# Two decode layers on one core: the order of the loads at the change of layers, and w4's last pieces

## The chip, the cores and the metric

One core of a Trainium2 chip. The metric is the device time of one execution in microseconds; below it also appears as the span, from the first to the last instruction in the trace.

## What is computed

One token passes through four steps: attention A, mixer B, A again, B again, with the same weights and the same K and V caches both times. So there are two layers of A and B, and everything is read from memory twice.

```python
# A: x (1,1,640); 32 heads of 192; the last W = 4096 of 32768 cached positions
q = (x @ wq).reshape(B, Sq, Hq, Dh) ...
k = k_cache[:, :, Sk - W:, :];  v = v_cache[:, :, Sk - W:, :]
p = softmax(einsum("bhqd,bhkd->bhqk", q, k) * Dh ** -0.5)
return einsum("bhqk,bhkd->bhqd", p, v) ... @ wo        # wo (6144, 640)
# B: with one position the four shifted parts are all zero, so hs = 0 and x1 = x
h2 = gelu(layernorm(x1) @ w3) @ w4                     # w3 (640, 1536), w4 (1536, 640)
return x1 + h2
# all: x = x + A(layernorm(x)); x = x + B(layernorm(x)); and both once more
```

## The kernel before

**Storage.** SBUF holds twelve cells of 1536 KB (128 partitions x 6144 bf16). A cell takes K or V of one head, or w3, w4 or a piece of wo. `take` (L147) gives the cell that has been free longest, `give` (L152) puts one back. Both run while the program is written, so the cell that a load gets is fixed, and so is the last reader of that cell's tenant before it, for which the load waits. Eight transposed K (heads 0 to 7) stay in their cells from layer 0 to layer 1, so layer 1 starts with work that needs no load. V of head 3 (`VC`) stays too. V of head 2 (`VP`) stays elsewhere, one part in PSUM: in layer 1 it has no load at all, but it needs a cell into which VectorE turns it back (`v_words`, L591, the transposes at L599). V of head 4 (`VX`) stays in part, so that layer 1 loads 864 KB of it. Most of w3 and w4 lies in a cell, the rest in a fixed tile `wx_sb` (one k-block of w3, three blocks of w4), which is loaded only in layer 0.

**Order of the loads.** All loads are issued by SyncE (SP), one after another, in the order of a written list, `layer_stream` (L246). `need` (L290) walks that list as far as the load asked for. An issue that waits holds up all behind it. Each transfer counts on one of eight counters in turn, so it also waits until the eighth transfer before it has landed.

**Change of layers.** Layer 0 ends with w3 and w4 in the mixer (`load_w3`, `load_w4`, `mixer`), then layer 1 begins. Its first takers of cells, in the order of the list, are v0 and v1 (V of heads 0 and 1), which get the cells of w3 and w4; then v2, then k8, v4 and k9. The scores of heads 0 to 3 (L494, called through `S`, L701) free one cell of a kept K each, in that order. In the kernel before, v2 gets head 0's cell, k8 head 1's, v4 head 2's; head 3's becomes a work area, and k9 gets head 4's.

**Computation.** TensorE makes the scores (L494), V's product (L610) and the projections; VectorE transposes K (L418) and the products (L617); ScalarE makes the exponentials. In the mixer, L942 multiplies by w3, L954 to L975 form the gelu, and L989 multiplies by w4: twelve blocks of five matmuls each. In layer 0 the order of the blocks is: eight in the cell, three in `wx_sb`, and last the ninth in the cell, a block of 160 KB that is loaded by itself (L238). L996 then makes x of the next layer. In layer 1 it is: the three in `wx_sb`, the eight in the cell, and the ninth; L994 makes the result, L1010 and L1012 turn it, and SP writes it (L1013).

Of the kernel before, what the change touches and what calls it, by code (L numbers as in the profile page):

```python
# [59 lines left out]
def kernel(  # L60
# [14 lines left out]
    nc = tc.nc  # L75
    shrink_ring(nc)
    _, _, D = A_x.shape
# [10 lines left out]
    QH = 4  # L88
# [17 lines left out]
    VC, VP, VX, VW, VN = 3, 2, 4, 20 * Dh // 2, (NKL + NKX) * Dh  # L106
    assert NA * D + FREE - 2 * VW <= FREE

    W3C, W4C = FREE // F, FREE // D
# [37 lines left out]
    def take(key):  # L147
        i = free.popleft()
        cell_of[key] = i
        return (low if i == NCELL - 1 else cells).tile([P, FREE], BF16, tag=f"cell{i}", name=f"cell{i}")  # L150
# [73 lines left out]
    def load_w4(layer):  # L224

        t = take(("w4", layer))
        nx, x0 = NF - W4C, (ND - W3C) * F
        pairs = B_w4.rearrange("(k p two) n -> p k (two n)", p=P, two=2)
        ones_ = B_w4.rearrange("(k p two) n -> p k two n", p=P, two=2)
        h = W4C // 2  # L230
        n = h if layer == 0 else h // 2
        for k in range(0, h, n):
            nc.sync.dma_start(t[:, 2 * k * D:2 * (k + n) * D].rearrange("p (k n) -> p k n", k=n),
                              pairs[:, 2 + k:2 + k + n, :])
        if layer == 0:
            nc.sync.dma_start(wx_sb[:, x0:x0 + 2 * D], pairs[:, 0, :])
            nc.sync.dma_start(wx_sb[:, x0 + 2 * D:x0 + 3 * D], ones_[:, 1, 0, :])
        nc.sync.dma_start(t[:, 2 * h * D:W4C * D], ones_[:, 1, 1, :])  # L238
        blocks = [wx_sb[:, x0 + k * D:x0 + (k + 1) * D] for k in range(nx)]
        blocks.append(t[:, 2 * h * D:W4C * D])  # L240
        blocks += [t[:, k * D:(k + 1) * D] for k in range(2 * h)]
        return blocks
# [3 lines left out]
    def layer_stream(layer):  # L246
        groups = GROUPS[layer]
        seq, later = [], []

        def k_item(hh):  # L250
            if layer == 0 or hh >= NKEEP:
                seq.append(("k", layer, hh))

        def v_item(hh):
            if (layer, hh) == (1, VC):
                return
            if (layer, hh) == (1, VP):
                later.append(("v", layer, hh))
                return
            seq.append(("v", layer, hh))  # L260

        if layer == 0:
            for hh in groups[0]:
                k_item(hh)
        for gi, cur in enumerate(groups):
            nxt = list(groups[gi + 1]) if gi + 1 < len(groups) else []
            late = gi + 2 >= len(groups)
            for i, hh in enumerate(cur):
                if nxt:
                    k_item(nxt.pop(0))  # L270
                if nxt and late and i == 2:
                    k_item(nxt.pop(0))
                v_item(hh)
                if later and i == QH - 1:
                    seq.append(later.pop())
                if layer == 0 and gi + 1 == len(groups) and i < 2:
                    seq.append(("wo", layer, groups[gi + i - 1][0] // QH))
            if gi + 2 < len(groups) and gi >= layer:
                seq.append(("wo", layer, cur[0] // QH))
        if layer == 1:  # L280
            for g in groups[-2:]:
                seq.append(("wo", layer, g[0] // QH))
        seq.append(("w3", layer))
        seq.append(("w4", layer))
        return seq

    stream = [("wq", 0, 0), ("x",)] + [("wq", 0, kc) for kc in range(1, ND)] + layer_stream(0) + layer_stream(1)
    pos = [0]

# [611 lines left out]
    def mixer(layer, x_cur, z, rs_cur, ss_cur, x_new, rs_new):  # L901
# [81 lines left out]
        y2_ps = psm.tile([P, ND], F32, tag="psm")  # L983
        n = NF - W4C
        fcs = list(range(n)), list(range(n + 1, NF))
        fcs = (fcs[1] + fcs[0] if layer == 0 else fcs[0] + fcs[1]) + [n]
        order = [(n, fc) for fc in fcs for n in range(ND)]
        for i, (n, fc) in enumerate(order):
            nc.tensor.matmul(  # L989
# [13 lines left out]
    zs = [const.tile([P, 1], F32, name=f"zs{i}") for i in range(4)]  # L1003
    attention(0, xT, rs0, x1, z[0], zs[0], zs[1])
    mixer(0, x1, z[0], zs[0], zs[1], x2, rs2)
    attention(1, x2, rs2, x3, z[1], zs[2], zs[3])
    mixer(1, x3, z[1], zs[2], zs[3], x4, None)

    row_ps = psm.tile([ND, P], out.dtype, tag="psm")
# [34 lines left out]
```

## Time and profile before

| what | value |
|---|---|
| median of three runs | 514.91 us (514.85 to 515.27) |
| the profiled execution | 513.87 us, span 512.1 us |
| TensorE busy | 326.1 us, 64% of the span; mean granted clock 0.682 |
| VectorE busy | 290.9 us, 57% |
| ScalarE busy | 48.8 us, 10% |
| DMA | 215.11 MB, mean 420 GB/s over the span |
| chain that ended last | wo 3.8% of the span, w4 2.0%, then L989, L994, L1010, L1012 |

How it is read: the page cuts the span into 40 slices of 12.8 us and gives for each the busy share of every engine in tenths, the clock that was granted to TensorE, the share of the 16 DMA engines and what they moved. Behind it stand questions to the trace: rows in order of time (start, duration, engine, line, operation, out<-in, number, and in brackets the idle time ahead of it with what ended it); the waits in total (engine, line, what was waited for: us in total, times, longest); and busy times by stretches. SPq is SP's DMA queue; the time of a transfer is given from issue to landing, and a transfer has landed when the last of the DMA engines has finished its part.

### The profile page before, as it was taken

The page shows a single profiled execution, that of the slowest core. Times are in us where ns is not written, and L with a number is a line of the kernel's source. Part 1 is how long each engine was busy: PE and PEld are TensorE (multiplying, and loading weights), DVE is VectorE, ACT ScalarE, POOL GpSimd, SP SyncE. Part 2 cuts the span into 40 slices and gives each one's busy share as a digit, 9 for nine tenths or more (in the row PEclk, how much of TensorE's full clock was granted, in tenths as well). Part 3 has the DMA queues.
Part 4 walks back from the last instruction along what each step waited for, and adds up shares of the span by engine and source line. Part 5 has one row for each costly group of instructions (what it writes and reads, how often), then busy time and mean ns, then how long its engine had stood idle before and what let it go on. Part 6 is the DMA issues. An engine that isn't in the chain of part 4 may idle for free. (4 is left out here: it accounts for less than half of the span.)

```text
span 512.1 us, 9455 instructions
## 1 busy us (share of the span) xinstructions
PE 326.1 (64%) x4084; PEld 191.4 (37%) x4084; DVE 290.9 (57%) x587; ACT 48.8 (10%) x173; POOL 4.0 (1%) x16
## 2 busy tenths in 40 slices
PE   1057657666566645857655767667676766767765
PEld 0023334333333323534333544434343443434435
DVE  2067667676565755467623245666576566756622
ACT  1000101010010100101011111001010100100011
POOL 2000000000000000000000000000000000000000
PEclk9999878567665776576675585675565577656765
DMA  8999999999999999999999999999999999999996
GB/s 369 430 430 427 432 439 430 439 427 415 454 433 427 434 408 425 430 416 451 428 403 417 351 444 427 424 436 420 434 427 420 430 439 427 424 439 430 419 407 240
DMA packets 11997, 215.11 MB, mean 420 GB/s; under 512 B 2548, under 2 KB 3060, under 8 KB 7412
## 3 DMA queue, kind: packets, MB, share of 16 engines
q1 hardware_dynamic: 11956, 214.51, 98.4%
q8 instruction: 32, 0.52, 0.4%
q14 instruction: 9, 0.07, 0.0%
HBM read 214.50 MB, written 0.00 MB: 419 GB/s over the span
## 5 line engine op out<-in xcount | busy, mean ns | idle before, releaser
L494 PE MATMUL ST_ps<-cell,Qblk 128*16 128x256 bf16 x1536 | 161.3, 378 | 102.7 <-DVE cell L418 67.9
L418 DVE STREAM_TRANSPOSE cell<-cell 128x768 uint32<-128x768 uint32 x224 | 200.4, 944 | 11.7 <-DMA cell<-in_A_k_cache_dram 11.5
L494 PEld LDWEIGHTS <-Qblk 128*16 128x16 bf16 x1536 | 84.7, 111 | 171.6 <-issue 145.8
L610 PE MATMUL O_ps<-cell,PT 128*2 128x384 bf16 x1010 | 101.5, 473 | 7.2 <-DMA cell<-in_A_v_cache_dram 5.2
L617 DVE STREAM_TRANSPOSE o_sb<-O_ps 128x384 f32<-128x384 f32 x64 | 37.2, 581 | 112.5 <-PE O_ps L610 112.3
L610 PEld LDWEIGHTS <-PT 128*2 128x2 bf16 x1024 | 46.5, 102 | 22.5 <-issue 13.6
L553 DVE STREAM_TRANSPOSE o_sb<-o_sb 128x256 bf16<-128x256 bf16 x16 | 7.1, 445 | 33.9 <-ACT o_sb L548 24.7
L625 ACT ACTIVATE oT<-oT_ps,rl 32x6 bf16<-32x6 f32 x40 | 10.3, 257 | 158.7 <-PE oT_ps L624 150.4
L624 PE MATMUL oT_ps<-o_sb,Lq 128*32 128x6 f32 x160 | 14.0, 196 | 11.2 <-DVE o_sb L617 10.6
L624 PEld LDWEIGHTS oT_ps<-o_sb,Lq 128*32 128x32 f32 x160 | 12.9, 145 | 21.7 <-issue 16.1
L630 ACT ACTIVATE oT<-oT_ps,rl 32x6 bf16<-32x6 f32 x24 | 6.2, 257 | 110.3 <-PE ST_ps L494 95.1
L448 PE MATMUL qT_ps<-xc,wq_sb 128*128 128x1 bf16 x210 | 7.2, 165 | 12.9 <-DMA wq_sb<-in_A_wq_dram 12.1
L437 PE MATMUL qr_ps<-wq_sb,xc 128*1 128x384 bf16 x90 | 13.5, 452 | 0.0
L564 PE MATMUL PT_ps<-o_sb,Eq 128*32 128x32 bf16 x256 | 7.2, 237 | 9.2 <-DVE o_sb L553 4.0
L462 DVE TENSOR_TENSOR Xq<-qT_ps,maskq 128x24 bf16<-128x24 f32 (+1 forms) x18 | 2.9, 159 | 17.9 <-PE qT_ps L448 17.5
L448 PEld LDWEIGHTS <-wq_sb 128*128 128x128 bf16 x210 | 6.8, 104 | 14.1 <-DMA wq_sb<-in_A_wq_dram 13.1
L569 PE MATMUL l_ps<-lh,ones 128*128 128x4 f32 x32 | 8.5, 336 | 4.9 <-ACT PT L567 4.9
L564 PEld LDWEIGHTS <-Eq 128*32 128x32 bf16 x256 | 5.4, 109 | 16.5 <-issue 16.4
L545 ACT COPY nb_sb<-nb_ps 128x1 f32<-128x1 f32 x16 | 2.5, 159 | 93.8 <-PE nb_ps L542 93.8
L656 PE MATMUL yr_ps<-cell,oT 128*1 128x320 bf16 x108 | 11.4, 357 | 0.0
L542 PEld LDWEIGHTS nb_ps<-ones,o_sb 1*128 1x128 f32 x32 | 7.3, 283 | 7.4 <-issue 5.5
L629 PE MATMUL oT_ps<-o,Lq 128*32 128x6 f32 x48 | 6.2, 201 | 6.0 <-DVE o L628 6.0
(146 smaller groups left out, 196.7 us busy)
## 6 DMA issues: line engine op xcount, KB each, us to landing
cell<-in_A_k_cache_dram SPq DMA_DIRECT2D x56, 1536.0 KB, 26.4
cell<-in_A_v_cache_dram SPq DMA_DIRECT2D x56, 1536.0 KB, 26.4
cell<-in_A_wo_dram SPq DMA_DIRECT2D x13, 960.0 KB, 24.5
wq_sb<-in_A_wq_dram SPq DMA_DIRECT2D x5, 1536.0 KB, 12.1
cell<-in_A_v_cache_dram SPq DMA_DIRECT2D x6, 768.0 KB, 23.1
cell<-in_A_v_cache_dram SPq DMA_DIRECT2D x2, 864.0 KB, 9.0
cell<-in_B_w_dram SPq DMA_DIRECT2D x1, 1536.0 KB, 11.8
cell<-in_B_w_dram SPq DMA_DIRECT2D x2, 768.0 KB, 10.2
```

Source lines behind the costliest of these rows:

```text
L418: nc.vector.transpose(Tu, Ku[:, :, q * NY:(q + 1) * NY])
L437: nc.tensor.matmul(qr_ps[32 * i:32 * i + 1, :], lhsT=xc[:, kc:kc + 1], rhs=wq_sb[:, kc, t0 * P + i * N:t0 * P + (i + 1) * N], start=(kc == ...
L448: nc.tensor.matmul(qT_ps[:, tl:tl + 1], lhsT=wq_sb[:, kc, t * P:(t + 1) * P], rhs=xc[:, kc:kc + 1], start=(kc == 0), stop=(kc == ND - 1))
L494: nc.tensor.matmul(ST_ps[r:r + QW, :].rearrange("p (g i) -> p g i", g=ng), lhsT=Q[:, n, :], rhs=T4[:, :, f, :, t], start=(hq == 0 and n == ...
L542: nc.tensor.matmul(nb_ps[:], lhsT=held["w"], rhs=ones[0:1, 0:1], start=True, stop=True)
L564: nc.tensor.matmul(PT_ps[32 * m:32 * (m + 1), :, :, ng * q:ng * (q + 1)], lhsT=Eq[:, q, :], rhs=src[:, m:QW:NM], start=True, stop=True)
L569: nc.tensor.matmul(l_ps[:], lhsT=ones[:], rhs=held["lh"][:], start=True, stop=True)
L610: nc.tensor.matmul(O_ps[r:r + 2, :], lhsT=PT[:, hq, 2 * i:2 * i + 2], rhs=v_pair(V, h, 2 * i * Dh, 2 * Dh), start=(i < 4), stop=(i >= NB - 4))
L617: nc.vector.transpose(o_sb[:], O_ps.rearrange("p (e a c) -> p e c a", e=2, c=NA))
L624: nc.tensor.matmul(oT_ps[r, :], lhsT=Lq[:], rhs=o_sb[:, e, :, e], start=(e == 0), stop=(e == 1))
L625: nc.scalar.activation(oT[r, :], oT_ps[r, :], ACTF.Copy, scale=rl[r, 0:1])
L656: nc.tensor.matmul(yr_ps[32 * i:32 * i + 1, :], lhsT=oT[:, k:k + 1], rhs=wo_t[:, k * D + i * N:k * D + (i + 1) * N], start=(k == 0), stop= ...
```

## The change

Three edits:

- In `layer_stream` the place of v2 in layer 1 moves: it was put behind the last head of the first group (heads 0 to 3), so ahead of k8, and now follows V of head 4. So k8 takes head 0's cell, v4 head 1's and v2 head 2's. As v2 has no load, the order of the issues stays; what changes is which cell each waits for.
- In layer 0 the load of w4's ninth block goes ahead of the two loads into `wx_sb`, and the matmuls follow: eight blocks in the cell, the ninth, then the three in `wx_sb`.
- In layer 1 w4's eight blocks come in three loads (640, 320 and 320 KB) where they came in two of 640 KB; the ninth block follows as before. The order of its matmuls is the same.

On TensorE the same 60 matmuls of the mixer stand in another order in layer 0; nothing else moves on TensorE, VectorE, ScalarE or GpSimd. SP has one issue more, in the last mixer.

```diff
@@ load_w4
         h = W4C // 2
-        n = h if layer == 0 else h // 2
-        for k in range(0, h, n):
+        k = 0
+        for n in (h,) if layer == 0 else (h - 2, 1, 1):
             nc.sync.dma_start(t[:, 2 * k * D:2 * (k + n) * D].rearrange("p (k n) -> p k n", k=n),
                               pairs[:, 2 + k:2 + k + n, :])
+            k += n
+        nc.sync.dma_start(t[:, 2 * h * D:W4C * D], ones_[:, 1, 1, :])
         if layer == 0:
             nc.sync.dma_start(wx_sb[:, x0:x0 + 2 * D], pairs[:, 0, :])
             nc.sync.dma_start(wx_sb[:, x0 + 2 * D:x0 + 3 * D], ones_[:, 1, 0, :])
-        nc.sync.dma_start(t[:, 2 * h * D:W4C * D], ones_[:, 1, 1, :])
@@ layer_stream
                 v_item(hh)
-                if later and i == QH - 1:
+                if later and seq[-1] == ("v", layer, VX):
                     seq.append(later.pop())
@@ mixer
         fcs = list(range(n)), list(range(n + 1, NF))
-        fcs = (fcs[1] + fcs[0] if layer == 0 else fcs[0] + fcs[1]) + [n]
+        fcs = fcs[1] + [n] + fcs[0] if layer == 0 else fcs[0] + fcs[1] + [n]
```

## The prediction

> **What bounds the kernel now.** I read the page's slices first, then the waits of the two computing engines by stretch, then the issues of SP's DMA queue, then the end. All times are of the profiled execution.
>
> ```profile
> DMA  8999999999999999999999999999999999999996
> GB/s 369 430 430 427 432 439 430 439 427 415 454 433 427 434 408 425 430 416 451 428 403 417 351 444 427 424 436 420 434 427 420 430 439 427 424 439 430 419 407 240
> ```
>
> The DMA engines are busy from end to end and mostly move 420 to 440 GB/s. The change takes away no byte, so it can only win where the stream falters: slice 22 (351 GB/s, 282 to 294 us) is the change of layers, the last slice is the end. Is the computation a second bound? This is every wait of TensorE and VectorE for a DMA between 286 us and the end:
>
> ```profile
> PEld L942 <- DMA cell<-in_B_w_dram: 0.9, 1, 0.9
> PE V_ps L942 <- DMA cell<-in_B_w_dram: 0.8, 1, 0.8
> PEld L989 <- DMA cell<-in_B_w_dram: 0.2, 1, 0.2
> PE y_ps L989 <- DMA cell<-in_B_w_dram: 0.2, 1, 0.2
> ```
>
> So in layer 1 the computation never waits for data until w3's second half. Two chains run side by side, **the transfers** and **the computation**; they meet at L942, where the transfers are 0.83 us late. This caps the case: whatever the seam gives to the transfers, the end moves by 0.83 us there and no further, because then the computation is the bound.
>
> The seam, by stretches (the last three columns are granted clock, DMA share, GB/s):
>
> ```profile
> 282.00:287.00 5.00, 2.70 (x71) 2.43 (x69) 2.08 (x16) 1.16 (x5) 0.00 (x0) 0.50 0.97 374
> 287.00:298.00 11.00, 9.75 (x239) 7.01 (x242) 3.57 (x12) 0.76 (x4) 0.00 (x0) 0.76 0.93 349
> 298.00:304.00 6.00, 3.87 (x86) 2.72 (x84) 2.21 (x10) 1.08 (x4) 0.00 (x0) 0.88 1.12 466
> 304.00:312.00 8.00, 5.76 (x72) 2.58 (x64) 1.78 (x4) 0.77 (x3) 0.00 (x0) 0.50 0.99 426
> ```
>
> Against the 426 GB/s that follow, 287 to 298 lost 11 x (1 - 349/426) = 2.0 us and 298 to 304 gave back 6 x (466/426 - 1) = 0.6: **1.4 us** net, as a mean over the engines.
>
> **What the change moves at the seam.** These are head 0's scores, the issues of v1, k8 and v4 (V and K of layer 1, by head), and head 1's and 2's scores:
>
> ```profile
> 285.93 0.33 SPq L156 DMA_DIRECT2D cell<-in_A_v_cache_dram  x1
> ...
> 288.28 1.46 PE L494 MATMUL ST_ps<-cell,Qblk 128*16 128x256 bf16 x24 [0.30 <-DVE Qblk L477]
> ...
> 289.80 1.46 PE L494 MATMUL ST_ps<-cell,Qblk 128*16 128x256 bf16 x24
> ...
> 291.30 0.33 SPq L156 DMA_DIRECT2D cell<-in_A_k_cache_dram  x1
> ...
> 291.70 1.15 PE L494 MATMUL ST_ps<-cell,Qblk 128*16 128x256 bf16 x24
> ...
> 292.90 0.33 SPq L181 DMA_DIRECT2D cell<-in_A_v_cache_dram  x1
> ```
>
> Each issue stands 0.04 to 0.05 us behind the end of the scores that free its cell: k8 behind head 1's (289.80 + 1.46 = 291.26), v4 behind head 2's (291.70 + 1.15 = 292.85). Head 0's cell goes to v2, which has no load: it is filled from PSUM by L599. After the change the three cells go to k8, v4, v2 in turn.
>
> 1. **k8** is issued behind head 0's scores: 288.28 + 1.46 + 0.04 = 289.78, or 1.52 us earlier. **v4** is issued behind head 1's, 291.30, or 1.60 earlier. Nothing is added to SP; k9 keeps its cell and its issue at 295.88, and so do all behind it.
> 2. **v2's** cell comes free at 292.85 and not at 289.74. L599 writes it at 294.82, behind the instruction before it on VectorE (L477, 294.64), so 1.97 us cover it; with the cover gone the softmax's first maximum (L519, 298.79) would be late behind it on VectorE after another 1.6 us.
> 3. **w4 of layer 0.** v1 waits for w4's cell: its waits are 1.6 us for w4's last block and then 0.3 for L989. The block that lands last there (160 KB, issued 275.44) now goes ahead of the 320 and 160 KB that are bound for another tile, and its five matmuls go ahead of those 15. The cell's last matmul ends 15 matmuls sooner (285.10 to 285.61: 0.51 us), so v1 is issued at about 285.4. The 60 matmuls stay 60; the 320 KB block lands behind 160 KB more, at about 284.75 + 0.4 = 285.15, and TensorE reaches it at 285.10 + 5 x 0.034 = 285.27. I cost this at nothing; with the cover of 0.12 gone x2, and so the computation, would be some 0.1 us late.
>
> How much do the transfers gain? By issue plus time to landing, k8 lands at 299.6 (291.30 + 8.3), v4 at 301.9, k9 at 305.6, v5 at 309.2: a full load takes 3.6 us in a full queue, v4's 864 KB 2.0. The trace has no k8 issued into this queue earlier, so I bound it. Upper end: v0, issued into a nearly empty queue, took 7.3 us; k9 by that row lands at 295.88 + 7.3 = 303.2 at the soonest, 2.4 us sooner. Lower end: only v1's shift counts, 0.5. A loss below nothing I exclude, since no load is issued later than before. I take **1.5 us**, the shift of k8 that v4 and k9 follow and near the 1.4 of the bytes. Does it last to the end? From 304.80 on loads land 15 us and more behind their issue (26.4 in the median), so the queue stays filled and a lead is kept. What arrives at the end is then 1.5 us, of which **0.83 us** count.
>
> **The end.** w4 of layer 1 came as 640, 640 and 160 KB and now comes as 640, 320, 320 and 160.
>
> ```profile
> 505.25 0.48 PE L942 MATMUL V_ps<-xc,cell 128*128 128x1 bf16 x12 [0.83 <-DMA cell<-in_B_w_dram]
> ...
> 507.63 0.67 PE L989 MATMUL y_ps<-hT,cell 128*128 128x1 bf16 x20
> ...
> 508.46 0.82 PE L989 MATMUL y_ps<-hT,cell 128*128 128x1 bf16 x25 [0.16 <-DMA cell<-in_B_w_dram]
> 509.32 0.16 DVE L994 TENSOR_TENSOR x<-base,y_ps 128x5 bf16<-128x5 f32 x1 [1.32 <-PE y_ps L989]
> ```
>
> Twenty-five matmuls stand behind the second 640 KB, which lands at 497.97 + 10.4 = 508.4. With it in halves, the first lands about 0.75 us sooner (half the 1.5 us between 506.9 and 508.4, the landings of the two 640 KB pieces), and ten matmuls x 0.033 fill the wait and run past 508.4. But TensorE is busy on both sides of the wait, so the gain is the wait alone, **0.16 us**, not the 0.33 of ten matmuls. The added issue costs SP 0.34 us beside the 9.8 us that it then waits for the result. A transfer is not issued before the eighth ahead of it has landed, so one more also pushes the last block one place on: it waits for the landing that SP's last instruction now waits 0.8 us for, and goes out at about 500.3 instead of 499.12. The rate holds until 504 us, so some 3.5 us cover it; uncovered it would cost 1.2.
>
> The 640 KB pieces land 1.5 us apart and the 160 KB block 0.4 behind the last (508.8), each at about 420 GB/s. So I see no price per transfer in a filled queue. The Trainium skill speaks against the change here: "DMA: Bandwidth & Descriptors", section "Anatomy of one DMA", puts about 2.0 us fixed on each transfer (for transfers issued from GpSimd), and its "Bandwidth" section asks for 1 MiB or more. By it the sum would be 1 us slower; the rows just given disagree with it.
>
> **Sum**: -0.83 - 0.16 = **-1.0 us** against the profiled 513.87 (span 512.1 and 1.8 around it). The median of the runs shown, 514.91, stands 1.0 above that execution; I take the same difference from it: **513.9**. A measurement of this kernel can tell about 0.2%, 1.03 us, from no change, so the forecast stands just at that line.
>
> **Rivals.**
> - *The seam gives little.* For it: the DMA share over 287 to 298 is 0.93, only 0.8 us idle, and v1's shift alone is 0.5. Then 0.3 to 0.6 us come through and 0.16 at the end: 514.2 to 514.5. Chance 0.20.
> - *The computation is already the bound in the runs that are timed*, which are 1.0 us longer than the profiled one. Then the seam is hidden and only the end is left: 514.75. Chance 0.12.
> - *The computation gets shorter*, because the clock's steps fall better on it. The granted clock in 286 to 296 is a mean of 0.68, in 296 to 303 it is 0.97; 24 score matmuls take 1.46 us in the slow part and 0.87 in the fast one (293.62). One step of some 3.4 us more at full clock is worth up to 1.4. With the transfers' 1.5 that ends near 513.2. Chance 0.10.
> - *Slower: the same clock falls worse.* The place is TensorE between 292 and 303 us, now at a mean clock of 0.97 and busy for 8.1 of the 11 us; 8.1 x (1.46/0.87 - 1) = 5.5 us are at stake. The computation has 0.83 us of slack, so slower begins where more than that plus 0.16 is lost, and by over 0.2% from 2.0 us on. Half of it lost gives 2.7 - 0.83 - 0.16 = +1.7: 516.6. Against it: the change moves no matmul there by more than 0.1 us. Chance 0.05. "TensorE: Matmul & The Clock Gate" in the Trainium skill, section "Part 1", says that the clock follows activity in free-running windows of 3.4 us; by that a step can fall otherwise in any execution, changed or not.
> - *Slower: each transfer has a fixed price at the end.* The nearest row is the result's write into an empty queue, 510.09 to 512.1: +2.0 - 1.0, 515.9. Chance 0.03; the landings 0.4 us apart speak against it. This is where the DMA page's rule would lead.
>
> **Chances and range.** Forecast 0.50, rivals 0.50 as given. Of the forecast about half (0.24) passes 1.03 us, which with the shorter computation makes faster 0.34; same is 0.26 + 0.20 + 0.12 = 0.58; slower 0.08. The range, 513.1 to 514.9, takes in all but the slower cases and the far part of the shorter computation.
>
> **What would show it.** k8's issue near 289.8, v4's near 291.3, v1's near 285.4, k9's unchanged near 295.9; over 350 GB/s between 287 and 298; k9 landed before 305; L942 with no wait for w3 or a short one; no wait inside the last 45 matmuls of L989. Wrong would be: issues moved but landings not (the loss isn't in the queue), or L942 still waiting 0.8 us (the lead was given back on the way).

## The result, and the profile after

The kernel after takes **512.81 us** (median of five runs, 512.72 to 514.16); before took 515.27 beside it (514.85 to 515.39). The ratio is **0.9967 with a 95% interval of 0.9952 to 0.9982**, so it is faster by 0.33%. The forecast was 513.9, in a range from 513.1 to 514.9: the median lies 0.3 us below the range; from the 514.91 that the forecast started from, this ratio leads to 513.2, inside it. Two more comparisons of the same kernel gave 0.9977 (0.9964 to 0.9990) and 0.9986 (0.9967 to 1.0004), with medians of 513.17 and 513.56. A ratio is not quite the quotient of the two medians beside it; where the two differ, the ratio is used. Weighted by their intervals the three ratios make 0.9976 (0.9967 to 0.9984), or 1.2 us.

The profiled execution of after is the 512.81 one, with a span of 511.0 us. Behind L236 its line numbers are one higher: L942 is now L943, L989 is L990, L638 is L639, L494 is L495. The slices of the page, for after:

```profile
DMA  8999999999999999999999999999999999999996
GB/s 369 431 431 428 433 440 431 440 428 415 444 433 401 435 428 441 431 407 457 429 391 417 380 438 432 421 428 441 432 425 431 432 424 431 428 426 435 424 403 246
```

The slice of the change of layers, which had 351 GB/s, now has 380; the others scatter, by up to 26 GB/s down and 21 up. The stretches of the seam (clock, DMA share, GB/s last) and SP's issues (start, duration; the first row holds v0 and v1, then k8, v4 and k9):

```profile
282.00:287.00 5.00, 2.65 (x71) 2.46 (x70) 2.10 (x16) 1.27 (x7) 0.00 (x0) 0.50 0.98 381
287.00:298.00 11.00, 9.24 (x246) 6.47 (x247) 3.54 (x11) 0.63 (x4) 0.00 (x0) 0.81 1.01 385
298.00:304.00 6.00, 3.87 (x86) 2.75 (x78) 2.21 (x10) 1.08 (x4) 0.00 (x0) 0.78 1.11 466
```

```profile
281.75 3.84 SPq L156 DMA_DIRECT2D cell<-in_A_v_cache_dram  x2
289.60 0.33 SPq L156 DMA_DIRECT2D cell<-in_A_k_cache_dram  x1
291.11 0.33 SPq L181 DMA_DIRECT2D cell<-in_A_v_cache_dram  x1
295.22 0.48 SPq L55 DMA_DIRECT2D cell<-in_A_k_cache_dram  x1
```

The issues stand where the prediction put them: k8 at 289.60 (289.78 foreseen), v4 at 291.11 (291.30), v1 at 285.27 by its own row (285.4). Only k9, foreseen unchanged at 295.88, went 0.66 us earlier, because the clock's step came earlier and the scores ahead of it were shorter (head 2's took 0.86 us for 1.15). In another profiled execution of after it went at 295.86. The stream between 287 and 298 us no longer falters: its share is 1.01 after 0.93.

Now the waits of TensorE and VectorE for a DMA from 286 us on, all of them, and the end of the kernel:

```profile
PEld L943 <- DMA cell<-in_B_w_dram: 1.2, 2, 1.0
PE V_ps L943 <- DMA cell<-in_B_w_dram: 0.9, 1, 0.9
PEld L639 <- DMA cell<-in_A_wo_dram: 0.4, 1, 0.4
PE y_ps L639 <- DMA cell<-in_A_wo_dram: 0.3, 1, 0.3
```

```profile
498.28 1.53 PE L639 MATMUL y_ps<-oT,cell 128*128 128x1 bf16 x45
500.08 0.70 PE L639 MATMUL y_ps<-oT,cell 128*128 128x1 bf16 x15 [0.28 <-DMA cell<-in_A_wo_dram]
...
504.24 0.48 PE L943 MATMUL V_ps<-xc,cell 128*128 128x1 bf16 x12 [0.92 <-DMA cell<-in_B_w_dram]
...
506.63 1.50 PE L990 MATMUL y_ps<-hT,cell 128*128 128x1 bf16 x45
```

The wait inside w4's last 45 matmuls is gone. But L943 still waits 0.92 us for w3's second half, although the transfers came 1 us sooner. So the computation came sooner as well: L639, the last output projection, begins at 498.28 and not at 500.43, and now waits for wo itself. The prediction had read the computation as a second bound that would stop the gain at 0.83 us. That is what the experiments had to settle. One more row belongs to the end, the write of the result, before and after:

```profile
510.09 0.30 SPq L1013 DMA_DIRECT2D out_dram<-Lb  x1
```

```profile
508.93 0.30 SPq L1014 DMA_DIRECT2D out_dram<-Lb  x1
```

From its issue to the end of the span it is 2.01 us before and 2.11 after.

### The profile page after: what moved, and what is told of

It is laid out like the page before. It is cut to its first block, busy times and chain, and to the rows that moved or that the text cites. A ratio compares the mean times of both kernels' runs of the same rounds, so it can differ in the third digit from the quotient of the medians.

```text
span 511.0 us, 9455 instructions
## 1 busy us (share of the span) xinstructions
PE 324.9 (64%) x4084; PEld 191.4 (37%) x4084; DVE 291.3 (57%) x587; ACT 48.9 (10%) x173; POOL 4.0 (1%) x16
## 4 chain that ended last, share of the span: by engine, by line
DMA 58%; PE 20%; DVE 17%; issue 2%; ACT 1%; SPq 1%; DVEq 0%; ACTq 0%
DMA cell<-in_A_k_cache_dram 34%; DMA cell<-in_A_v_cache_dram 20%; DVE cell L419 12%; PE ST_ps L495 9%; PE O_ps L611 6%; DMA cell<-in_B_w_dram 4%; DVE o_sb L618 2%; PE qT_ps L449 1%; PE y_ps L990 1%; DVE pm L520 1%; PE nb_ps L543 1%; DVE o_sb L554 1%; PE l_ps L570 1%; PE pmT_ps L525 1%; DVE V_ps L600 1%
## 5 line engine op out<-in xcount | busy, mean ns | idle before, releaser
L495 PE MATMUL ST_ps<-cell,Qblk 128*16 128x256 bf16 x1536 | 161.8, 379 | 101.8 <-DVE cell L419 66.7
L495 PEld LDWEIGHTS <-Qblk 128*16 128x16 bf16 x1536 | 85.0, 111 | 171.4 <-issue 145.0
```

Of the source, the lines that this page charges most:

```text
L495: nc.tensor.matmul(ST_ps[r:r + QW, :].rearrange("p (g i) -> p g i", g=ng), lhsT=Q[:, n, :], rhs=T4[:, :, f, :, t], start=(hq == 0 and n == ...
```

## The experiments

**Theory A**: the transfers set the end, and the gain is the lead that they take at the change of layers. **Theory B**: the computation sets the end in the runs that are timed, and after is faster because TensorE's clock falls better on it.

The table puts the profiled executions beside each other. The first two columns of numbers are the stream's rate and TensorE's granted clock between 287 and 298 us. "k10" is the mean landing, over the 16 DMA engines, of K of head 10, the second K load behind k8; "mean" and "last" are the landings of w3's second half over the 16 engines (a transfer has landed with the last); the start is that of the matmuls that wait for it, at L942 in before; the last column is the span less that start.

| profiled execution | GB/s | clock | k10 | mean | last | start (wait) | span | span less start |
|---|---|---|---|---|---|---|---|---|
| before | 349 | 0.76 | 311.0 | 503.4 | 505.2 | 505.25 (0.83) | 512.1 | 6.8 |
| before, again | 337 | 0.78 | 311.6 | 503.8 | 506.8 | 506.85 (0.93) | 513.7 | 6.9 |
| cells only | 366 | 0.79 | 310.4 | 502.8 | 504.1 | 504.17 (0.56) | 511.1 | 6.9 |
| w4 of layer 0 only | 365 | 0.78 | 310.8 | 503.3 | 505.2 | 505.26 (1.21) | 512.0 | 6.7 |
| cells and w4 of layer 0 | 374 | 0.82 | 310.2 | 502.7 | 504.1 | 504.17 (0.92) | 511.0 | 6.9 |
| last pieces only | 325 | 0.70 | 311.8 | 504.2 | 507.0 | 507.09 (0.92) | 513.9 | 6.8 |
| cells later | 308 | 0.50 | 312.0 | 504.5 | 506.2 | 506.20 (0.88) | 513.1 | 6.9 |
| after | 385 | 0.81 | 310.2 | 502.7 | 504.2 | 504.24 (0.92) | 511.0 | 6.8 |
| after, again | 374 | 0.53 | 310.9 | 503.4 | 505.8 | 505.85 (0.93) | 512.7 | 6.8 |
| after, third | 428 | 0.78 | 310.1 | 502.5 | 505.4 | 505.47 (0.93) | 512.3 | 6.8 |
| after, less load | 381 | 0.75 | 310.0 | 500.6 | 502.4 | 504.45 (none) | 511.1 | 6.6 |
| after, less computation | 377 | 0.51 | 311.8 | 504.2 | 505.7 | 505.74 (0.92) | 512.5 | 6.8 |
| after, both less | 367 | 0.53 | 311.3 | 501.9 | 504.1 | 504.13 (0.92) | 510.9 | 6.8 |

In all rows but one, w3's second half starts at most 0.1 us behind its landing, and the kernel ends 6.7 to 6.9 us later. One landing sets the end; the exception is the run with fewer bytes.

The table also shows that a lead from the seam arrives whole. From k10's mean landing to w3's the stream takes 192.3 to 192.5 us in all eleven rows with all bytes, whatever the kernel and the clock, and 190.6 us in the two with 768 KB less. What is gained or lost up to k10 is still there 192 us later.

### The cells alone

```diff
-                if later and i == QH - 1:
+                if later and seq[-1] == ("v", layer, VX):
```

> Only the twelfth cell changes hands. Theory A (the lead of the transfers at the change of layers does it): k8 issued near 289.8 and v4 near 291.3 with v1 still near 285.9; the stream over 287 to 298 us rises from 349 towards 375 GB/s; w3's second half lands 0.6 to 0.9 us sooner and the time falls by most of what the whole change gave, 1.2 to 1.8 us. Theory B (the computation of layer 1 bounds the timed runs and the change only happened to meet better clock steps): issues move as said, but the time stays within 0.5 us of before.

Measured: 514.38 us against 515.06 before, ratio 0.9991 (0.9972 to 1.0010): no difference that can be told, and less than the 1.2 to 1.8 us that theory A had led to expect; this timing alone fits theory B as well. In the trace k8 went at 289.92, v4 at 291.43 and v1 at about 286.07, so the rewired cells do what the diff says. By the means over the engines, k9 landed at 303.06 after 303.66 and 304.08 in the two profiles of before.

### w4's block in layer 0 alone

```diff
+        nc.sync.dma_start(t[:, 2 * h * D:W4C * D], ones_[:, 1, 1, :])
         if layer == 0:
...
-        nc.sync.dma_start(t[:, 2 * h * D:W4C * D], ones_[:, 1, 1, :])
...
-        fcs = (fcs[1] + fcs[0] if layer == 0 else fcs[0] + fcs[1]) + [n]
+        fcs = fcs[1] + [n] + fcs[0] if layer == 0 else fcs[0] + fcs[1] + [n]
```

> Only w4's order in layer 0. Theory A: v1 issued 0.5 us sooner (285.4), k8 and v4 unchanged at 291.3 and 292.9, so the queue still runs short before k8; 0.0 to 0.4 us faster. Theory B: no change, within 0.3 us; x2 no later than 0.1 us.

Measured: 514.30, ratio 0.9984 (0.9969 to 0.9999). v1 went at 285.41, as foreseen, k8 at 291.30 as before. With v1 half a microsecond earlier and nothing else, 287 to 298 had 365 GB/s for 349 or 337, as much as with the cells. The gain of 0.8 us by the ratio is more than either theory expected (0.4 at most).

### Both edits of the seam, with the old last pieces

The two diffs above together.

> The twelfth cell and w4's order in layer 0 together, with w4's old pieces at the end. Theory A: v1, k8 and v4 issued as in the changed kernel, the stream over 287 to 298 us at 380 to 390 GB/s, and all of the gain of the whole but the 0.16 us of the last pieces. If the parts only add up as they did singly (0.7 and 0.8 us, each barely clear of noise), 1.4 us faster; if v1's earlier issue is worth more once k8 follows closely, up to 2. Theory B: within 0.7 us of before.

Measured: 513.64 against 514.37 before, ratio 0.9984 (0.9969 to 0.9999); the whole change ran at 513.17 beside it. The profiled execution has the span of after's, 511.0 us, and keeps the wait at the end:

```profile
506.55 0.67 PE L989 MATMUL y_ps<-hT,cell 128*128 128x1 bf16 x20
507.38 0.83 PE L989 MATMUL y_ps<-hT,cell 128*128 128x1 bf16 x25 [0.16 <-DMA cell<-in_B_w_dram]
```

The last matmul here ends 4.04 us behind the start of w3's second half (507.38 + 0.83 - 504.17), in after 3.89 (506.63 + 1.50 - 504.24). So at the last matmul the smaller pieces are worth 0.15 us, as the wait said. At the end of the span most of it is gone: from the issue of the result's write to the end it is 2.01 to 2.03 us in the six profiles with the old pieces and 2.11 to 2.13 in the seven with the new ones. The packed traces show why: at the end SP waits for its counters in five waits of a fixed order, about 0.06 us each; with one load more the write counts on the next of the eight counters, which moves from the last of these waits to the third. So some 0.05 us of the 0.15 are left, and the seam is the rest. The timed gain of 0.8 us lies between what the two theories expected (1.4 or more, and under 0.7).

### The last pieces alone

```diff
-        n = h if layer == 0 else h // 2
-        for k in range(0, h, n):
+        k = 0
+        for n in (h,) if layer == 0 else (h - 2, 1, 1):
...
+            k += n
```

> Only w4's smaller last pieces in layer 1. Theory A: the 0.16 us of wait inside L989 go, the issues and landings ahead of it stay; 0.1 to 0.2 us faster. Rival (a fixed price per transfer): the last block lands later than 508.8 - 508.4 = 0.4 us behind the piece ahead of it, and the time rises by up to 1 us.

Measured: 515.72 against 515.06, ratio 1.0007 (0.9990 to 1.0024): neither a gain nor a price that a timing shows. In its trace the pieces landed at 508.7, 509.5, 510.2 and 510.6: 320 KB 0.7 to 0.8 us behind the piece ahead, 160 KB 0.4. All 1440 KB of w4 took 3.59 us behind w3, as they do in before with one load fewer (505.20 to 508.79); so the added load costs the stream nothing.

### The seam made worse

The work area, which before takes head 3's cell, is put ahead of k8 in the list, so that k8 and v4 each get a cell one head later; k9 keeps its own. Nothing else changes in the computation. The line that does it (the loader that takes the cell is left out here):

```diff
                     seq.append(later.pop())
+                    seq.append(("area", layer))
```

> The suspected cost made larger: from the kernel before, the work area takes its cell ahead of k8, so k8 waits for head 2's scores (issued near 292.9 where it was 291.3) and v4 for head 3's (near 294.6 where it was 292.9); k9 and all behind it as before. Theory A: the stream over 287 to 298 us falls below 340 GB/s, k9 lands 1 to 1.6 us later, and the time rises by 0.8 to 1.6 us. Theory B: within 0.4 us of before.

Measured: 515.14 against 514.37, ratio 1.0010 (0.9998 to 1.0022). The issues of k8 and v4 went to 292.95 and 295.23, and the stream fell:

```profile
287.00:298.00 11.00, 10.35 (x206) 6.47 (x206) 3.54 (x11) 0.57 (x4) 0.00 (x0) 0.50 0.85 308
```

The clock stood at 0.50 here, for 0.76 in before, and this is why k9, whose cell did not change, went at 297.18. That doesn't explain the rate: after, again, had 374 GB/s at a clock of 0.53 and with k9 at 297.29.

With the stream's rate the mean landing of w3 falls in order: 308 GB/s and 504.5 here; 325 and 504.2, 337 and 503.8, 349 and 503.4 with the old seam; 365 and 503.3 with w4's block, 366 and 502.8 with the cells, 374 and 502.7 with both. That is theory A's order; the three profiles of after (385, 374 and 428 with 502.7, 503.4 and 502.5) lie at its end, with a scatter of their own. Less computation (377 and 504.2) breaks it: there k9 was issued only at 297.82, and 298 to 304 had 420 GB/s, where after had 466. The timed loss of 0.5 us is not separated from nothing; theory A had expected 0.8 to 1.6.

### Before, once more

No edit; one execution.

> The kernel before once more, for a second profile of it: its profiled execution took 513.87 us where its other runs take 514.85 to 515.39. Theory A: the extra 1.0 to 1.5 us are lost in the transfers at the change of layers (w3's second half lands later than 505.2 by that much, and L942 still waits for it). Theory B: they are in the computation (L942 waits less than 0.3 us or not at all, its first part ends later than 504.4).

Measured: 515.62 us, 1.75 longer than the profiled execution of before. Its waits for a DMA from 286 us on, the largest of each line:

```profile
DVE cell L418 <- DMA cell<-in_A_k_cache_dram: 1.8, 1, 1.8
PEld L942 <- DMA cell<-in_B_w_dram: 1.2, 2, 1.0
PEld L638 <- DMA cell<-in_A_wo_dram: 1.1, 2, 0.7
PEld L610 <- DMA cell<-in_A_v_cache_dram: 0.9, 1, 0.9
```

So in another execution of the same kernel layer 1 does wait for K, V and wo: there the computation is ahead of the transfers, and not abreast of them. What differs is the clock. The same stretch, before and then before again (TensorE's busy time first; clock, DMA share and GB/s last):

```profile
384.00:404.00 20.00, 12.69 (x134) 6.74 (x128) 12.25 (x21) 1.03 (x4) 0.00 (x0) 0.50 0.99 424
```

```profile
384.00:404.00 20.00, 12.04 (x138) 6.82 (x131) 13.72 (x23) 1.03 (x4) 0.00 (x0) 0.76 0.99 426
```

At a clock of 0.50 one group of four heads (L542 to L542) took 30.3 us (375.8 to 406.1), at 0.76 it took 27.6 (376.6 to 404.2). Of the thirteen profiled executions three had 0.50 here (before, cells only, after with less load), and just these three run L638's sixty matmuls without a wait for wo. The others had 0.55 to 0.79; they include after and before again.

### After, twice more

No edit.

> The changed kernel once more, on the chip of the next three and against the same runs of the kernel before: the whole to which the parts are added. Theory A (transfers bound the end, the lead from the change of layers arrives there): 1.2 to 2.0 us faster than before. Theory B (the first comparison was lucky in its steps of the clock): under 0.7 us.

> The kernel after once more, on the same chip as the two beside it, so that they have their own base. Against the kernel before: ratio 0.995 to 0.998 by its two comparisons so far (0.9967 and 0.9977). Theory A: in whatever execution is profiled, L943 waits 0.5 us or more for w3's second half, and the time follows that landing: time = landing of w3's second half + 8.6 us (504.2 and 512.81 in the first profile of it). Theory B: in the longer executions the wait is gone.

Measured: 513.17 against 514.37, and 513.56 against 515.14, the ratios given above. The profiled executions took 514.44 and 514.13, and both still wait 0.93 us for w3 at L943, so the wait isn't lost in longer executions; by the landing plus 8.6 us they should take 514.4 and 514.0. The second ratio, 1.2 us, stands at the lower edge of what theory A had led to expect. The third, 0.9986, lies above the 0.995 to 0.998 that were expected, though its interval reaches into them.

The table shows what else moved the lead. Of the seven profiles with both edits of the seam, four had a clock of 0.75 to 0.82 between 287 and 298 us: k9 went at 295.1 to 295.9 and k10 landed, by the mean, at 310.0 to 310.2. In the other three the clock was 0.51 to 0.53: k9 went at 297.3 to 297.8, behind scores that took longer, and k10 landed at 310.9 to 311.8, as with the old seam (311.0 to 311.8, at 0.70 to 0.78). So at a like clock the two edits bring k10 1.3 us forward (310.1 for 311.5), and a slow clock at the seam can take nearly all of it away again, through the issues and not through the computation at the end.

### Less computation, fewer bytes, and both

The first leaves out half of the V product in heads 28 to 31 of layer 1. The second loads only half of V of head 16 in layer 1 (`HALF = 16`), and the product reads that half twice (its line is left out here). The third does both. The edits, in after:

```diff
+            if layer == 1 and h >= 28 and 4 <= i < NB - 4:
+                continue
...
+        if (layer, h) == (1, HALF):
+            nc.sync.dma_start(t[:, 0:FREE // 2], src[:, 0:FREE // 2])
+            return t
```

> The kernel after, with half of the V product's matmuls (L611, the middle eight of sixteen) left out in heads 28 to 31 of layer 1; all loads stay. The trace of after has 16 such matmuls at 1.45 us a head in the last 12 us before out_proj, so this takes about 0.7 us from each of four heads, some 2 to 3 us of the computation's last part. Transfers are the bound (theory A): the time stays that of the kernel after within 0.3 us, and L943's wait for w3's second half is at least as long as after's 0.92 us, or the wait for wo at L639 grows (0.28 in after) and x2 still comes no more than 1 us sooner. Computation is the bound in the timed runs (theory B): 1 to 2.5 us faster than the kernel after.

> The changed kernel with V of head 16 in layer 1 loaded by half only (768 KB less, about 1.8 us of a full stream; V's product for that head takes the first half twice, so that part of the computation is not the reference's, and the work of every engine stays). Theory A, transfers bound the end: 1.5 to 1.9 us faster than the changed kernel. The rival of the prediction, that the computation caps the end: w3's second half lands that much sooner but L942 no longer waits for it, and the time falls by 0.9 us at most.

> The kernel after, with only half of V of head 16 of layer 1 loaded (768 KB less; the product reads the loaded half twice) and, as in the run beside it, half of the V product's matmuls left out in heads 28 to 31. The bytes are 768 KB / 420 GB/s = 1.9 us. The run that left out these bytes alone ended with w3 landed ahead of the computation and fell only 0.7 us. If the computation stood right behind the transfers (theory A with the cap that the prediction named, only later), taking both away gives about the whole 1.9 us: 1.5 to 2.2 us below the kernel after run beside it, with L943 waiting for w3 again or with no wait and TensorE's last part earlier by over 1 us. If something else than these two chains limited that run, it stays at 0.5 to 1 us below.

Measured, **less computation**: 514.32 us, where after beside it took 513.56 and before 515.14. Against before that is 0.9983 (0.9968 to 0.9997), against after's 0.9986; no gain at all. The freed time turned into waits for wo and w3:

```profile
499.58 0.56 PE L641 MATMUL y_ps<-oT,cell 128*128 128x1 bf16 x15 [0.19 <-DMA cell<-in_A_wo_dram]
500.76 0.56 PE L641 MATMUL y_ps<-oT,cell 128*128 128x1 bf16 x15 [0.61 <-DMA cell<-in_A_wo_dram]
501.60 0.70 PE L641 MATMUL y_ps<-oT,cell 128*128 128x1 bf16 x15 [0.28 <-DMA cell<-in_A_wo_dram]
...
505.74 0.48 PE L945 MATMUL V_ps<-xc,cell 128*128 128x1 bf16 x12 [0.92 <-DMA cell<-in_B_w_dram]
```

Theory B falls: it had expected 1 to 2.5 us less than after. **Fewer bytes**: 512.47 against 514.37 before (0.9950, 0.9931 to 0.9968) and 513.17 after. 768 KB are 1.9 us at 420 GB/s; by the ratios 1.4 of it came through (0.9950 against 0.9977), by the medians 0.7, so between what theory A and the computation as a bound had led to expect. In its trace w3 landed 1.8 us sooner than in after, and the computation, here with the slow clock, came last:

```profile
500.59 1.76 PE L643 MATMUL y_ps<-oT,cell 128*128 128x1 bf16 x60
503.65 0.46 PE L947 MATMUL V_ps<-xc,cell 128*128 128x1 bf16 x12
...
504.45 0.46 PE L947 MATMUL V_ps<-xc,cell 128*128 128x1 bf16 x12
```

**Both less**: 512.06 (0.9958, 0.9945 to 0.9971), 1.5 us below after beside it by the medians and 1.4 by the ratios, the lower edge of what was expected, with L949 waiting 0.92 us again. By the ratios that is no more than fewer bytes alone, so the timings don't show a cap by the computation; one trace does. There the computation is the next bound, behind the transfers, at a distance that the clock changes from one execution to the next: in the profiled execution of after it is 1.2 us (the waits of 0.28 at wo and 0.92 at w3), with the clock at 0.50 and w3 1.8 us sooner it was used up.

## Why the prediction was right or wrong

- **What moves at the seam**: right. k8, v4 and v1 went 1.70, 1.79 and 0.66 us earlier (1.52, 1.60 and 0.5 foreseen), and SP got nothing to do for it. v2's later cell cost nothing that a trace shows. k9's 0.66 is the clock's doing; "its issue at 295.88" held only for a like clock (297.3 to 297.8 in three profiles).
- **How much the transfers gain**: the mechanism was right, the size was off. The step that failed is "I take 1.5 us, the shift of k8 that v4 and k9 follow". By the last of the 16 engines k9 did land 1.9 us sooner (303.6 for 305.5); by their mean only 0.8 (302.82 for 303.66; 1.3 against before again). At w3, by the same means, 0.8 (502.65 for 503.43), and over three profiles with the old seam and three of after 1.0 (503.8 and 502.9). The count of bytes, which the prediction took as its support and not as its result, comes near: between these two profiles 11 x (385 - 349) / 426 = 0.9 us more moved in 287 to 298, and nothing given back more in 298 to 304 (466 both times); over the three of each, 1.5 us more moved and 0.7 given back. What the step left out is the clock: k10 came 1.3 us sooner at a like clock, and 0.5 (310.9 for 311.5) in after's execution at 0.53.
- **"They meet at L942 ... because then the computation is the bound"**: wrong, and it is the step that failed in kind. The wait of 0.83 us was taken for the distance between two independent chains. It is nearly a constant: in the ten profiles in which L638 itself waited for wo, of old and new seam, it is 0.88 to 0.93 nine times and 1.21 once. In after the last wo matmuls start at 500.08, behind their landing, and the mixer could use w3's second half at 502.86 + 0.46 = 503.32; w3 lands 0.9 later because it stands behind wo in the same stream. Both ends of that wait are set by the transfers and move together. The profiled execution of before looked otherwise: its clock stood at 0.50 for 20 us, and its output projection began without a wait for wo.
- **The test named for a wrong prediction**, "L942 still waiting 0.8 us (the lead was given back on the way)", misled for the same reason: the wait stayed and the lead arrived.
- **The end**: half right. The wait inside L989 is gone, L990 ends 0.15 us sooner, and the added piece costs the stream nothing. But it sets the result's write on another counter, and SP's waits behind the write then take 0.1 us longer, which the prediction put at nothing: some 0.05 us are left of the 0.16. The row speaks against about 2.0 us fixed for each transfer, which the Trainium skill gives in "DMA: Bandwidth & Descriptors", section "Anatomy of one DMA", for another way of issuing: behind others, 160 KB took 0.4 us.
- **The sum**: -1.0 us foreseen, -1.2 measured over three comparisons. That the two are close is luck, because errors met: a gain of 1.5 was cut to 0.83 by a cap that was not there, where about 1.0 came through whole, and the end gave less than its 0.16. The median of 512.81 that fell out of the range belongs to the comparison with the largest gain of the three; the medians of the other two, 513.17 and 513.56, lie inside it.
- **The rivals**: that the seam gives little is refuted by the stream's rate; that the computation bounds the timed runs by the kernel with less of it; a shorter computation by the clock did occur (498.28 for 500.43), but before has it too in its second profile (0.76 for 0.50 over 20 us), and the end didn't follow it. The slower clock at the seam occurred also, in three of seven profiles with both edits. It cost those executions most of their lead, by later issues and not, as the rival had it, by a computation that becomes the bound.
- **Open**: why the last engine in one execution trails the mean by 1.3 us and in another by 3.0. How often the clock at the seam is slow in the timed runs, and whether the change makes that likelier: none of the five profiles with the old seam or one of its two edits had it, three of the seven with both did, and twelve profiles are too few to tell. The two seam edits are worth 0.5 and 0.8 us by their ratios, and together 0.8; their intervals don't tell how they add.

## What to carry to other kernels

A wait for a transfer is not slack between computation and transfers when the computation stood waiting for an earlier transfer of the same stream: then both ends of the wait shift together, and the whole lead arrives. Whether two chains are abreast should be read from more than one execution, since a clock that stood at half speed in one stretch can make a computation look like a bound. A lead in a filled queue is best sized by the mean landing over all engines of a load behind the stretch, or by the bytes moved up to there, not by the moment when one transfer's slowest engine ends. And a stretch in which computation frees the cells for the next loads should be compared at the same clock: the issues follow it.

## What was not expected of the hardware

- The engines of one stream don't end together. The first of the sixteen finished w3's second half at 500.5 to 502.6 us with all bytes loaded, the last 3.1 to 5.1 us later, and the end follows the last. Before ranged from 513.7 to 517.3 us over 29 runs on one chip, more than the change is worth. In before and before again the first engine ended 0.3 us apart (501.5 and 501.8), the last 1.6.
- TensorE's clock differs for a long stretch between executions of one program: 0.50 and 0.76 over the same 20 us, with 30.3 and 27.6 us for a group of heads. The Trainium skill, "TensorE: Matmul & The Clock Gate", section "Part 1", has windows of 3.4 us that run freely and so fall differently in each run; the trace agrees that it differs by run, and shows that the difference can last for several such windows.
